# A 96-byte gap that moves the x tiles, chunk 0's weights and the staging tiles of a fused attention and feed-forward kernel

## The chip, the cores and the metric

The kernel runs on one core of one Trainium2 chip. The metric is the device time of one execution in microseconds (us). Three runs of the kernel before took 732.08, 733.01 and 733.45 us; the median is 733.01 us.

## The reference

Attention over 4 batches, 8 heads, 576 positions and a head size of 64, with a bias that a small network computes from the relative position, and behind it a feed-forward layer over the 2304 tokens of 512 values:

```
x_rel = log1p(|i - j|) / log1p(max(i, 1))
bias  = relu(x_rel * w1 + b1) @ w2                 # hidden size 32, one value per head
p     = softmax(q @ k.T / sqrt(64) + bias)
x     = (p @ v), heads side by side                # 2304 x 512, float32
h     = x @ w_in                                   # 512 -> 2048
out   = max(0.01 * h, h) @ w_out                   # 2048 -> 512
```

## The kernel before, in words

The first 318 us compute the bias and the attention; the change doesn't move an operand of TensorE in them. What follows is the feed-forward layer, and that is where the moved tiles are read.

**How it is tiled.** The 2304 tokens are cut into five blocks (`BLOCKS`, L31): blocks 0 to 3 of 512 tokens, block 4 of 256. The 2048 inner values are cut into 16 chunks of 128 (`m`). A pair (n, m) is block n, chunk m. `ffn1(n, m)` (L432 to L442) makes one chunk of h: 12 matmuls, each of which streams a tile of x (512 columns, 256 in block 4) through a stationary 128x128 piece of w_in. `ffn2(n, m)` (L458 to L469) adds the chunk to the output: for each 128 tokens three matmuls (L467, L468, L469), which stream 512 columns of w_out through a stationary piece of the activated chunk, 12 matmuls in a block of 512 tokens and 6 in block 4.

**Why three matmuls for one product.** Every float32 operand is held as two float32r tiles, a high part and the rest: `xh`, `xl` for x, `wih`, `wil` for w_in, `woh`, `wol` for w_out, `gh`, `gl` for the activated chunk. A product is high·high, high·rest and rest·high.

**Order.** The loop at L565 issues for j = 0, 1, ...: `ffn1` of pair j, its activation (`ffn_act`, two ScalarE instructions at L449 and L450, and `ffn_lo`, one VectorE instruction at L456), then `ffn2` of pair j - 2. So TensorE does 12 matmuls of `ffn1`, then 12 of `ffn2` of two pairs earlier, and so on. Ahead of each matmul its weights are loaded (LDWEIGHTS, in the profile the engine PEld); the load for the next matmul starts together with the current one.

**Weights.** All 16 chunks of weights stay in SBUF from block 0 on. While block 0 runs, VectorE and ScalarE still unpack and split the chunks 2 to 15 (`w_abs`, `w_bits`, `w_hi`, `w_lo`, through the staging tiles `raw` and `tmp`): this work stands between the activations of block 0 in the same queues. It is the list `todo` at L542.

**Where the tiles lie.** SBUF has, in each partition, tiles at byte addresses that the pools hand out. The pools on the right side grow downwards from the top. At step n = 8 of the attention (L496 to L503) the pool `gen` is closed, and three pools are opened on the right: `early` (x tiles of even blocks, `x_alloc(early, 0)`, and chunk 0's weights, `w_alloc(early, 0)`), and below it `stage` and `stage_y` (the staging tiles). When the staging is done, the pool `late` takes its place below `early` with the x tiles of odd blocks. The weights of chunks 1 to 14, the `g`, `gh` and `gl` tiles and chunk 15's weights come from pools on the left side, whose first byte is fixed by what lies there. In the kernel before the addresses are, as remainders of the division by 256 and by 512:

| tiles | address of the first | mod 256 | mod 512 |
|---|---|---|---|
| x of even blocks (`xh00`) | 204768 | 224 | 480 |
| x of odd blocks (`xh10`) | 188384 | 224 | 480 |
| weights of chunk 0 (`wih0`) | 221152 | 224 | 480 |
| staging `raw`, `tmp` | 184288, 196576 | 224 | 480 |
| weights of chunks 1 to 15 (`wih1`) | 45184 | 128 | 128 |
| `gh`, `gl` (`gh0`) | 161920 | 128 | 128 |

Every tile of a row is a multiple of 2048 bytes long (staging `raw` 4096), so all of a row have the first one's remainders. A piece of 128 stationary columns begins at a multiple of 512 bytes in its tile, a streamed operand at its tile's first byte. So in `ffn1` of chunk 0 both operands of a matmul have remainder 224, in `ffn1` of the other chunks x has 224 and the weights 128; in `ffn2` of chunk 0 the streamed weights have 224 and the stationary `gh`, `gl` 128, and in `ffn2` of the other chunks both have 128.

The two attention operands of L230 serve as a comparison further on: `qs` (stationary) lies at 66176 and 71296, both 128 mod 512; `ks1` alternates from one unit (a batch and a pair of heads) to the next between 82560 and 87424, which are 128 and 384 mod 512, and `ks2` likewise.

Of the kernel before, what the change touches and what calls it, by code (L numbers as in the profile page):

```python
# [8 lines left out]
F32 = mybir.dt.float32  # L9
# [26 lines left out]
def attention_ffn(ctx: ExitStack, tc: tile.TileContext, qt, kt, vm, vt, wi, wo, cst, out):  # L36
# [37 lines left out]
    def gen_setup():  # L74
        cut = 214 + S - 16 * GEN[0]
        for c in (slice(0, cut), slice(cut, 214 + S)):
            nc.sync.dma_start(out=cs[:, c], in_=cst[:, c])
        nc.vector.memset(warm[:], 0.0)
        nc.scalar.activation(out=warm[:], in_=warm[:], func=AF.Exp)
        nc.vector.tensor_scalar(out=bps[:], in0=psib, scalar1=b1c, scalar2=None, op0=ALU.mult)  # L80
        for c in (slice(0, cut - 214), slice(cut - 214, S)):
            nc.vector.tensor_scalar(out=ltw[:, c], in0=ltw[:, c], scalar1=w1c, scalar2=None, op0=ALU.mult)
        nc.gpsimd.tensor_scalar(out=w2d, in0=w2d, scalar1=8.0, scalar2=None, op0=ALU.mult)
# [60 lines left out]
    def gen_tick(g):  # L144
        if g + 1 < 36:
            gen_r(g + 1)
        if 0 <= g < 36:
            gen_mm(GEN[g])
        if 0 <= g - 1 < 36:
            gen_ev(GEN[g - 1])  # L150
        for c in {16: "0", 24: "1", 27: "M", 34: "2", 37: "3"}.get(g, ()):
            load_bias(0, c)
# [19 lines left out]
    def load_unit(u):  # L172
        hp, b = divmod(u, B)
        q_, k_ = raw_b[u % 2]
        for p in (0, 64):
            nc.sync.dma_start(out=q_[p:p + 64], in_=qt[hp, b])
            nc.sync.dma_start(out=k_[p:p + 64], in_=kt[hp, b])
        raw[u] = (q_, k_)

    def load_v(u):  # L180
        hp, b = divmod(u, B)
        v_ = ap.tile([128, 4, 128], F32, tag="v", name="v", bufs=3)
        nc.sync.dma_start(out=v_[:], in_=vm[hp, b])
        for h in range(2):
            nc.sync.dma_start(out=vt_b[u % 3][64 * h:64 * h + 64, h, :], in_=vt[hp, b, h])
        vv[u] = v_

    def split_hi(u, what):
        q_, k_ = raw[u]
        if what == "q":  # L190
            qs = qs_b[u % 2]
            nc.vector.tensor_copy(qs[:].rearrange("p (a c) -> p a c", a=2)[:, :, 0:S], q_[:].rearrange("p (a c) -> p a c", a=2))
            ks1 = ap.tile([128, KW], F32R, tag="ks1", name="ks1", bufs=2)
            ks2 = ap.tile([128, KW], F32R, tag="ks2", name="ks2", bufs=2)
            qk[u] = (qs, ks1, ks2)
        else:
            nc.vector.tensor_copy(qk[u][1][:], k_[:])
# [175 lines left out]
    def w_alloc(pool, m):  # L373
        wt[m] = [pool.tile([128, DM], F32R, name=f"w{c}{m}") for c in ("ih", "il", "oh", "ol")]

    def x_alloc(pool, i):
        for k in range(KC):
            xs[i, k] = [pool.tile([128, BLK], F32R, name=f"x{c}{i}{k}") for c in "hl"]
# [46 lines left out]
    def w_split(m):  # L425
        for i in range(2):
            w_hi(m, i)
            w_lo(m, i, nc.vector)
# [50 lines left out]
    with tc.manual_schedule():  # L479
        gen_setup()  # L480
        for u in range(2):
            load_unit(u)
            load_v(u)
        sp_ops = [(u, w, a) for u in range(1) for w, a in (("q", None), ("q", 0), ("q", 1), ("k", None), ("k", 0), ("k", 1))]
        done = -1
        early_ops = []
        for n in range(NTILE + LAG + 6):
            u, i = divmod(n, 9)
            if u == 0:
                while done < GEN_AT[i]:  # L490
                    gen_tick(done)
                    done += 1
                    if done >= 6 and done % 2 == 0 and sp_ops:
                        w = sp_ops.pop(0)
                        split_hi(*w[:2]) if w[2] is None else split_lo(*w)
            if n == 8:  # L496
                gen.close()
                early = ctx.enter_context(tc.tile_pool(name="early", bufs=1, side="right"))
                x_alloc(early, 0)
                w_alloc(early, 0)  # L500
                stage, stage_y = ExitStack(), ExitStack()
                pools["s"] = stage.enter_context(tc.tile_pool(name="stage", bufs=1, side="right"))
                pools["y"] = stage_y.enter_context(tc.tile_pool(name="stage_y", bufs=1, side="right"))  # L503
            step(n)
            if n == 13:
                w_fill()
                for m in range(5):
                    early_ops += [(w_abs, m, h) for h in range(2)]
                    early_ops += [(w_bits, m, h, k) for k in range(4) for h in range(2)]
                    if m == 0:  # L510
                        early_ops += [(w_hi, 0, h) for h in range(2)] + [(w_lo, 0, h, nc.vector) for h in range(2)]
            for _ in range({0: 2, 4: 2}.get(i, 0) if n >= 18 else 0):
                if early_ops:
                    f, *args = early_ops.pop(0)
                    f(*args)
            if n == NTILE + 2:
                ffn1(0, 0)
            if u < HP * B:
                if u % B == B - 1 and u // B + 1 < HP:
                    c = {1: "0", 2: "1", 3: "M", 4: "2", 6: "3"}.get(i)  # L520
                    if c:
                        load_bias(u // B + 1, c)
                if u + 1 < HP * B:
                    for f, *args in SPL.get(i, ()):
                        (split_hi, split_lo)[f](u + 1, *args)
                if i == 0 and u + 2 < HP * B:
                    load_unit(u + 2)
                if i == 8 and u + 2 < HP * B:
                    load_v(u + 2)
        att.close()  # L530
        fp = ctx.enter_context(tc.tile_pool(name="ffn", bufs=1, reuse_waits="tile"))
        for m in range(1, MF - 1):
            w_alloc(fp, m)
        for c in ("g", "gh", "gl"):
            gt[c] = [fp.tile([128, BLK], F32 if c == "g" else F32R, name=f"{c}{i}") for i in range(1 if c == "g" else 3)]
        w_split(1)

        def more():
            stage_y.close()
            w_alloc(ctx.enter_context(tc.tile_pool(name="last", bufs=1, reuse_waits="tile")), MF - 1)  # L540

        todo = []  # L542
        for m in range(2, 5):
            todo += [(0, w_hi, m, i) for i in range(2)] + [(0.69, w_lo, m, i, nc.vector) for i in range(2)]
        todo.append((0, more))
        halves_ = [(m, i) for m in range(5, MF) for i in range(2)]
        todo += [(0, w_abs, *t) for t in halves_[:2]]
        for j, t in enumerate(halves_):
            todo += [(0.42, w_bits, *t, 0), (0.43, w_bits, *t, 1)]
            if j:  # L550
                todo.append((0.69, w_lo, *halves_[j - 1], nc.vector))
            todo += [(0.69, w_bits, *t, 2), (0.69, w_bits, *t, 3)]
            todo.append((0, w_hi, *t))
            if j + 2 < len(halves_):
                todo.append((0, w_abs, *halves_[j + 2]))
        todo.append((0.69, w_lo, *halves_[-1], nc.vector))

        def work(budget):
            while todo and budget > 0:
                cost, f, *args = todo.pop(0)  # L560
                f(*args)
                budget -= cost

        seq = [(n, m) for n in range(len(BLOCKS)) for m in range(MF)]
        for j in range(len(seq) + 2):  # L565
            if j < len(seq):
                n, m = seq[j]
                if j:
                    ffn1(n, m)
                work(2.6)  # L570
                ffn_act(n, m)
                work(2.6)
                ffn_lo()
                if (n, m) == (0, MF - 3):
                    assert not todo
                    stage.close()
                    lp = ctx.enter_context(tc.tile_pool(name="late", bufs=1, side="right", reuse_waits="tile"))
                    x_alloc(lp, 1)
                    x_split(1, 0)
                if n + 1 < len(BLOCKS) and m >= MF - (4 if n else 3):  # L580
                    x_split(n + 1, m - MF + 4)
            if j >= 2:
                ffn2(*seq[j - 2])
# [41 lines left out]
```

## Time and profile before

| | |
|---|---|
| median of three runs | 733.01 us |
| profiled execution, from its first to its last instruction | 731.9 us |
| TensorE, matmuls | 710.1 us, 97% of the span |
| VectorE | 394.1 us, 54% |
| ScalarE | 365.6 us, 50% |
| GpSimd | 127.0 us, 17% |
| DMA | 68.26 MB, 93 GB/s over the span |

The page gives for the profiled execution its span, 731.9 us, and no other time of its own; the median of the runs is 1.1 us above it. A matmul's end in the trace is modelled, and matmuls overlap: the duration of one (some 393 ns for 512 columns) is longer than the step from its start to the next one's. How fast TensorE goes is read from the starts.

### The profile page before, as it was taken

To read this page: it belongs to the slowest core of one execution; us is meant where nothing else is said; L and a number is where in the kernel's file an instruction comes from. 1 tells how busy PE (TensorE), PEld (TensorE's weight loads), DVE (VectorE), ACT (ScalarE), POOL (GpSimd) and SP (SyncE) were. 2 spreads that over 40 slices of the span, in tenths; PEclk is the share of its full clock that TensorE was granted. 3 is DMA by queue.
4 is the path that set the end of the run, shared out by engine and by line. 5 is a ranking of instruction groups with operands and counts; after the bars stand their busy time and mean duration, and the time that the engine had idled before them with its cause. 6 is when DMAs were issued, how large, how long until landed. Compare 5 with 4: busy or idle time off the path is not lost.

```text
span 731.9 us, 11398 instructions
## 1 busy us (share of the span) xinstructions
PE 710.1 (97%) x4192; PEld 556.2 (76%) x4192; DVE 394.1 (54%) x1012; ACT 365.6 (50%) x808; POOL 127.0 (17%) x167
## 2 busy tenths in 40 slices
PE   6998999999999999998999999999999999999998
PEld 2347688778878887866877888888888888888896
DVE  7996789789888889759997211122111221112111
ACT  7797777777877777665555221222221231122221
POOL 2104545445544454200000000000000000000000
PEclk9999999999999999999999999999999999999999
DMA  9798848537627950104551010000000010000100
GB/s 211 253 317 229 216 112 243 125 97 218 171 68 183 244 151 18 58 1 144 175 176 52 1 57 1 1 0 28 30 1 1 0 58 1 0 1 0 59 1 30
DMA packets 30263, 68.26 MB, mean 93 GB/s; under 512 B 8192, under 2 KB 8320, under 8 KB 30208
## 3 DMA queue, kind: packets, MB, share of 16 engines
q1 hardware_dynamic: 30208, 67.54, 32.6%
q8 instruction: 33, 0.54, 0.3%
q14 instruction: 22, 0.18, 0.1%
HBM read 51.92 MB, written 15.61 MB: 92 GB/s over the span
## 4 chain that ended last, share of the span: by engine, by line
PE 78%; DVE 15%; DMA 3%; issue 1%; ACT 1%; SPq 0%; POOL 0%; DVEq 0%; POOLq 0%
PE ps_o L441 12%; PE ps_t L441 11%; PE ps_o L335 10%; PE ps_s L230 10%; PE ps_s L468 8%; PE ps_s L467 8%; PE ps_s L469 8%; PE ps_t L295 6%; DVE p L252 2%; DVE tmp L411 2%; DVE tmp L413 2%; DMA raw<-qt 2%; PE ps_o L123 2%; PE ps_t L123 1%; DVE wol L423 1%
## 5 line engine op out<-in xcount | busy, mean ns | idle before, releaser
L456 DVE TENSOR_TENSOR gl<-g,gh 128x512 fp32r<-128x512 f32 (+1 forms) x80 | 51.0, 638 | 270.5 <-ACT g L450 270.5
L230 PE MATMUL ps_s<-ks,qs 128*128 128x288 f32 x640 | 120.3, 314 | 4.5 <-DVE mx L252 4.5
L467 PE MATMUL ps_s<-woh,gh 128*128 128x512 f32 x288 | 113.3, 393 | 1.6 <-ACT g L450 1.6
L469 PE MATMUL ps_s<-woh,gl 128*128 128x512 f32 x288 | 113.1, 393 | 0.9 <-DVE gl L456 0.6
L468 PE MATMUL ps_s<-wol,gh 128*128 128x512 f32 x288 | 113.5, 394 | 0.0
L252 DVE CUSTOM_DVE_ANT_0 p<-ps_s,bias 128x576 f32<-128x576 f32 x128 | 95.0, 751 | 25.9 <-PE ps_s L230 23.1
L260 ACT ACTIVATE p<-p,mx 128x576 f32<-128x576 f32 x128 | 99.9, 780 | 12.9 <-DVE mx L252 11.1
L230 PEld LDWEIGHTS ps_s<-ks,qs 128*128 128x128 f32 x640 | 89.5, 189 | 20.3 <-DVE mx L252 6.4
L311 ACT COPY PT<-ps_t 128x512 f32<-128x512 f32 x128 | 73.7, 577 | 37.5 <-PE ps_t L295 37.5
L449 ACT ACTIVATE gh<-ps_o 128x512 fp32r<-128x512 f32 (+1 forms) x39 | 21.5, 551 | 127.8 <-PE ps_o L441 127.8
L449 ACT ACTIVATE gh<-ps_t 128x512 fp32r<-128x512 f32 (+1 forms) x39 | 21.5, 551 | 114.4 <-PE ps_t L441 114.2
L295 PE MATMUL ps_t<-ident,p 128*128 128x128 f32 x512 | 77.0, 273 | 0.9 <-ACT PT L311 0.8
L335 PE MATMUL ps_o<-PT,v 128*64 128x288 f32 x512 | 69.2, 412 | 0.0
L469 PEld LDWEIGHTS ps_s<-woh,gl 128*128 128x128 f32 x288 | 54.1, 188 | 15.5 <-DVE gl L456 3.5
L467 PEld LDWEIGHTS ps_s<-woh,gh 128*128 128x128 f32 x288 | 54.1, 188 | 14.0 <-ACT g L450 2.0
L295 PEld LDWEIGHTS ps_t<-ident,p 128*128 128x128 f32 x512 | 61.7, 140 | 2.6 <-ACT PT L311 1.8
L468 PEld LDWEIGHTS ps_s<-wol,gh 128*128 128x128 f32 x288 | 54.1, 188 | 11.6
L441 PE MATMUL ps_o<-xh,wil 128*128 128x512 f32 (+1 forms) x156 | 58.4, 375 | 0.0
L441 PE MATMUL ps_t<-xh,wil 128*128 128x512 f32 (+1 forms) x156 | 58.3, 374 | 0.0
L441 PE MATMUL ps_o<-xl,wih 128*128 128x512 f32 (+1 forms) x156 | 58.2, 373 | 0.0
L441 PE MATMUL ps_t<-xl,wih 128*128 128x512 f32 (+1 forms) x156 | 58.2, 373 | 0.0
L441 PE MATMUL ps_o<-xh,wih 128*128 128x512 f32 (+1 forms) x156 | 58.0, 372 | 0.0
(98 smaller groups left out, 1111.8 us busy)
## 6 DMA issues: line engine op xcount, KB each, us to landing
raw<-kt SPq DMA_DIRECT2D x32, 304.0 KB, 5.9
raw<-qt SPq DMA_DIRECT2D x32, 288.0 KB, 5.1
raw<-wi SPq DMA_DIRECT2D x16, 512.0 KB, 3.6
raw<-wo SPq DMA_DIRECT2D x16, 512.0 KB, 3.6
scr<-x SPq DMA_DIRECT2D x21, 295.5 KB, 4.4
bias<-scr SPq DMA_DIRECT2D x16, 288.0 KB, 5.4
out<-x SPq DMA_DIRECT2D x18, 256.0 KB, 2.1
v<-vm SPq DMA_DIRECT2D x16, 256.0 KB, 4.2
```

The costliest lines, as they stand in the source:

```text
L230: nc.tensor.matmul(s_[:, S0 + HS * hh:S0 + HS * hh + HS], qs[:, c0:c0 + 128], ks[:, k0 + HS * hh:k0 + HS * hh + HS], start=(j == 0), stop= ...
L252: nc.vector.tensor_tensor_reduce(out=p, in0=s_[:, S0:S0 + S], in1=bt, scale=-0.125, scalar=3.4e38, op0=ALU.add, op1=ALU.min, accum_out=i)
L260: nc.scalar.activation(out=p, in_=p, func=AF.Exp, bias=i, scale=-1.0, accum_out=sm)
L295: nc.tensor.transpose(t0[:, 128 * jb:128 * jb + 128], p[:, p0 + 128 * jb:p0 + 128 * jb + 128], ident[:])
L311: nc.scalar.copy(out=PT[u, g][:, 0:8, c].rearrange("p (j h) c -> p j h c", h=2)[:, :, h, :], in_=t0[:].rearrange("p (j c) -> p j c", j=4))
L335: nc.tensor.matmul(o[64 * h:64 * h + 64, 0:HS], l, r, start=(jb == 0), stop=(jb == 4))
L441: nc.tensor.matmul(h_[:, :N], w, x[:, :N], start=(j == 0), stop=(j == len(mms) - 1))
L449: nc.scalar.activation(out=gh[:, :N], in_=h_[:, :N], func=AF.Prelu, alpha=0.01)
L456: nc.vector.tensor_sub(gl[:, :N], g[:, :N], gh[:, :N].bitcast(F32))
L467: nc.tensor.matmul(o, gh[:, c], wt[m][2][:], start=(m == 0), stop=False)
L468: nc.tensor.matmul(o, gh[:, c], wt[m][3][:], start=False, stop=False)
L469: nc.tensor.matmul(o, gl[:, c], wt[m][2][:], start=False, stop=(m == MF - 1))
```

## The change

One line is added: a tile of 24 float32 (96 bytes in each partition) in the pool `early`, behind x and chunk 0's weights. No instruction reads or writes it. The pool grows by 96 bytes, so its tiles, and all that lies below it on the right side, begin 96 bytes lower. Nothing else is changed: each engine's instructions stand in the same order as before, with the same waits.

```
                 early = ctx.enter_context(tc.tile_pool(name="early", bufs=1, side="right"))
                 x_alloc(early, 0)
                 w_alloc(early, 0)
+                early.tile([128, 24], F32, name="gap")
                 stage, stage_y = ExitStack(), ExitStack()
```

The addresses after it; rows that aren't here stay as they were:

| tiles | address of the first | mod 256 | mod 512 |
|---|---|---|---|
| x of even blocks (`xh00`) | 204672 | 128 | 384 |
| x of odd blocks (`xh10`) | 188288 | 128 | 384 |
| weights of chunk 0 (`wih0`) | 221056 | 128 | 384 |
| staging `raw`, `tmp` | 184192, 196480 | 128 | 384 |

## Rows read from the trace of the kernel before

**Rows 1.** The page: span, busy time of two engines, granted clock in 40 slices.

```profile
span 731.9 us, 11398 instructions
...
PE 710.1 (97%) x4192; PEld 556.2 (76%) x4192; DVE 394.1 (54%) x1012; ACT 365.6 (50%) x808; POOL 127.0 (17%) x167
...
PEclk9999999999999999999999999999999999999999
```

**Rows 2.** Windows: stretch, its length, busy us of each engine, clock, DMA share.

```profile
410.00:499.10 89.10, 89.10 (x385) 72.15 (x384) 14.78 (x22) 20.58 (x38) 0.00 (x0) 1.00 0.03 12
```

**Rows 3.** Chain of waits, pieces of L441 in blocks 1 to 3: start, us, what.

```profile
493.75 2.81 PE ps_o L441 x12
...
499.33 2.77 PE ps_t L441 x12
...
504.86 2.81 PE ps_o L441 x12
...
510.44 2.82 PE ps_t L441 x12
...
516.05 2.80 PE ps_o L441 x12
...
521.61 2.81 PE ps_t L441 x12
...
588.49 2.77 PE ps_t L441 x12
```

**Rows 4.** Timeline of PE at the very end: start, us, instruction.

```profile
723.98 0.39 PE L467 MATMUL ps_s<-woh,gh 128*128 128x512 f32 x1
...
726.06 0.39 PE L467 MATMUL ps_s<-woh,gh 128*128 128x512 f32 x1
...
726.74 0.39 PE L467 MATMUL ps_s<-woh,gh 128*128 128x512 f32 x1
...
727.42 0.39 PE L467 MATMUL ps_s<-woh,gh 128*128 128x512 f32 x1
```

**Rows 5.** Windows over block 0, columns as in rows 2.

```profile
325.00:394.60 69.60, 67.00 (x280) 52.15 (x281) 67.98 (x128) 39.49 (x70) 0.00 (x0) 1.00 0.47 144
394.60:409.80 15.20, 15.20 (x68) 12.29 (x67) 6.42 (x10) 6.60 (x13) 0.00 (x0) 1.00 0.00 1
```

**Rows 6.** Timeline in block 0, VectorE and the weight load behind it.

```profile
390.13 0.68 DVE L456 TENSOR_TENSOR gl<-g,gh 128x512 fp32r<-128x512 f32 x1
...
390.87 0.19 PEld L469 LDWEIGHTS ps_s<-woh,gl 128*128 128x128 f32 x1 [0.51 <-DVE gl L456]
```

**Rows 7.** Timeline of PE in block 4, first matmuls of chunks.

```profile
677.50 0.28 PE L441 MATMUL ps_t<-xh,wih 128*128 128x256 f32 x1
...
678.93 0.39 PE L467 MATMUL ps_s<-woh,gh 128*128 128x512 f32 x1
...
681.69 0.28 PE L441 MATMUL ps_o<-xh,wih 128*128 128x256 f32 x1
...
683.13 0.39 PE L467 MATMUL ps_s<-woh,gh 128*128 128x512 f32 x1
```

**Rows 8.** Timeline at the start of ffn2 in block 1: eviction and first matmul.

```profile
422.03 0.59 ACT L474 COPY x<-ps_s 128x512 f32<-128x512 f32 x1 [0.45 <-DVE x L476]
423.92 0.39 PE L467 MATMUL ps_s<-woh,gh 128*128 128x512 f32 x1
```

**Rows 9.** VectorE groups between 318 and 420 us: busy us, mean ns.

```profile
L456 DVE TENSOR_TENSOR gl<-g,gh 128x512 fp32r<-128x512 f32 x18 | 12.4, 688 | 17.7 <-ACT g L450 17.7
L423 DVE TENSOR_TENSOR wol<-tmp,woh 128x512 fp32r<-128x512 f32 x15 | 10.3, 686 | 0.7 <-ACT woh L419 0.7
```

**Rows 10.** Waits of engines for the staging DMA: us in total, times, longest.

```profile
ACT tmp L400 <- DMA raw<-wo: 3.5, 10, 0.6
```

**Rows 11.** Windows of L230 alone in two neighbouring units: PE, PEld busy.

```profile
86.30:102.20 15.90, 7.54 (x40) 5.58 (x40) 1.00 0.40 98
102.20:118.10 15.90, 7.52 (x40) 5.60 (x41) 1.00 0.72 192
```

More of the change, by code (lines that the diff above doesn't have):

```diff
@@ L500, in attention_ffn @@
                 w_alloc(early, 0)
+                early.tile([128, 24], F32, name="gap")
                 stage, stage_y = ExitStack(), ExitStack()
```

## The prediction

> **What bounds the kernel now.** I read the page first, to see whether an engine is full: the matmuls are busy for 97% of the 731.9 us, and the granted clock is full (the 2.4 GHz level) in all 40 slices [rows 1]. The windows come next, since a share over the whole span mixes stages. In block 1 TensorE is busy for all of 89.10 us, VectorE for 14.78 and ScalarE for 20.58 [rows 2]; blocks 2 and 3 read alike. So in these blocks nothing but the step from one matmul to the next sets the time. The chain of waits shows these steps by chunk: the reader is to see that one `ffn1` chunk in 16 is shorter. Twelve matmuls take 2.81 us in nearly every chunk, but 2.77 us in (2, 0) and (3, 0), at 499.33 and 588.49 [rows 3]. Chunk 0 is the only one whose w_in has the remainder of x, 224 mod 256 and 480 mod 512. `ffn2` is what lies between two such pieces. Behind 499.33 + 2.77 it takes 2.76 us, and behind 516.05 + 2.80 again 2.76: streamed w_out and stationary `gh`, `gl` agree there. Behind 510.44 + 2.82 it takes 2.79 us: that is `ffn2` of (2, 0), whose w_out has 224 against 128 [rows 3]. Two kinds of matmul, with different tiles and different absolute addresses, tell the same: agreeing operands are faster.
>
> How fast agreeing operands can be is seen where they last longest. The kernel ends with three `ffn2` chunks in a row, 18 matmuls that all agree. The first nine steps, from 723.98 to 726.06, take 2.08 us, 0.231 each; the next six, from 726.06 to 727.42, take 1.36 us, 0.2267 each [rows 4]. So the steps are uneven behind a matmul that disagrees and settle after nine. In block 1 to 3 no run of agreeing matmuls is longer than 12, so they hardly reach the settled state before the next `ffn1` disturbs them. Disagreeing ones cost 2.81/12 = 0.234.
>
> **The change part by part.** The order of the instructions and their waits are the same on every engine; only addresses move.
>
> *Blocks 1 to 3.* Modulo 256, x goes from 224 to 128, where the weights of chunks 1 to 15 are; w_out of chunk 0 goes to 128, where `gh` is. If agreement modulo 256 is what counts, all 384 matmuls of a block agree, with no disturbance from 410.00 to 677.50. A block takes 588.49 - 499.33 = 89.16 us [rows 3]. At the settled step it takes 384 x 0.2267 = 87.05 us. Gain 2.11 us per block, 6.33 us for three. The settled step does hold over a border between chunks: of the 18 matmuls at the end the 13th, at 726.74, is the first of chunk (4, 15), and the steps on both sides of it are 0.227 [rows 4].
>
> *Block 0.* A faster matmul gives nothing while TensorE waits for VectorE. From 325.00 to 394.60 VectorE is busy for 67.98 of 69.60 us, the rest being the short steps between its instructions [rows 5]; it unpacks and splits weights and makes `gl` in the same queue. The last wait for it ends at 390.87: a weight load was idle for 0.51 us until `gl` of (0, 10), begun at 390.13, was there [rows 6]. Whatever TensorE gains before that becomes a longer wait at this place. From 390.87 to 410.00 it runs freely, 19.13 us; at the same rate, 19.13 x 2.11/89.16 = 0.45 us.
>
> *Block 4.* Its `ffn1` streams 256 columns. Chunk 0 (agreeing) takes 678.93 - 677.50 = 1.43 us, chunk 1 (not agreeing) 683.13 - 681.69 = 1.44 us [rows 7]. So matmuls of this width show nothing, and I take 0 for them. The 512-wide matmuls here are 24 of block 3's last two `ffn2` chunks and 96 of block 4, 120 in all. If they settled they would save 120 x (0.231 - 0.2267) = 0.5 us; if the 256-wide ones between them disturb them as now, nothing. I take 0.3, nearer to the upper end as 24 + 18 of them have others of 512 columns ahead.
>
> *What else moves.* The staging tiles go from 224 to 128. The VectorE group with mixed remainders (`wol` from `tmp` at 224 and `woh` at 128) takes 686 ns, the one with all at 128 688 ns [rows 9]: VectorE doesn't respond, cost 0, at most 2 ns x 100 instructions = 0.2 us either way. The staging DMAs write to lower addresses; ScalarE waits 3.5 us in total for them, at most 0.6 at once [rows 10], and this lies beside VectorE's full queue. Bounds for that: 0 to 0.5 us lost. Nothing in the attention reads a moved tile on TensorE: 0.
>
> *What is late next.* At a block's end the accumulators are copied out; the last copy begins at 422.03 and takes 0.59, and the next `ffn2` begins at 423.92 [rows 8]. A faster `ffn1` ahead of it takes 0.1 us of the 1.3 us between. No new wait follows. The copies and the store behind the last matmul stay as they are.
>
> *A rule against it.* The Trainium skill (SBUF — State Buffer, section "Who interferes with whom") gives TensorE two independent read ports, one for the streamed operand and one for weight loads, and says that TensorE waits on nobody. By that, relative addresses are worth nothing, the sum is 0 and the time 733.0 us. The trace doesn't agree: 2.77 against 2.81 us for the same matmuls [rows 3].
>
> **The sum.** 6.33 + 0.45 + 0.3 = 7.1 us. The profiled execution would go from 731.9 to 724.8 us. The median of the runs is 1.1 us above the span, which I keep: 733.0 - 7.1 = 725.9 us.
>
> **The rivals.**
>
> 1. *The period is longer than 256.* All agreeing pairs that this trace holds agree modulo 512 too. After the change x has 384 mod 512 and the weights of chunks 1 to 15 128: half a period apart, should 512 be what counts. `ffn1` would stay at 2.81 us and the time at 733.0 us. Against it stand the attention's matmuls at L230. From one unit to the next `ks` changes from 128 to 384 mod 512 against a fixed `qs`, and 40 matmuls take 7.54 and 7.52 us [rows 11]. That is weak, since these stream 288 columns and the 256-wide ones show no response to a disagreement either [rows 7].
>
> 2. *Addresses aren't the cause.* Something else makes the first chunk of a block quick. Then nothing changes: 733.0 us. Against it: `ffn1` of chunk 0 is quicker than its neighbours and `ffn2` of chunk 0 is slower than its own [rows 3], as agreement has it and as no common cause at a block's start would.
>
> 3. *Each chunk unsettles the next.* The operands agree, but the change between x and w_out starts the uneven steps anew. `ffn1` then takes 2.77 instead of 2.81 us, `ffn2` stays at 2.76. In 89.16 us that is 15 x 0.04 + 0.03 = 0.63 us; from 390.87 to 677.50, 3.2 such blocks, 2.0 us: 731.0 us. For it: every run of 12 starts unevenly now. Against it: the chunk border in rows 4.
>
> 4. *Slower: a remainder of 256 modulo 512 disturbs more than 96 modulo 256 did.* The place is `ffn1` of chunks 1 to 15, 48 of them behind 390.87. No row shows this distance with 512 columns. If the loss against the settled step doubles, from 0.2342 - 0.2267 = 0.0075 to 0.015 us, each chunk takes 0.09 us more: 48 x 0.09 = 4.3 us, 737.3 us. It decides from the point where an `ffn1` step is above 0.2342 on average. For it only speaks that the distance is unseen; against it rows 11.
>
> **How the numbers follow.** The forecast has 0.62: agreement has two independent witnesses, and of the periods that fit them (64, 128, 256, 512; 32 or less doesn't fit, 96 being its multiple) only 512 makes the change miss. Rival 1 has 0.16, rival 2 0.06, rival 3 0.07, rival 4 0.09. A measurement of this kernel tells about 0.2%, 1.5 us, from no change. Forecast and rival 3 are faster: 0.69; rivals 1 and 2 the same: 0.22; rival 4 slower: 0.09. The forecast's own range is 724.6 us (all of block 4 and 1 us of scatter between runs) to 727.2 us (none of block 4, half of block 0, 0.5 lost to staging and the rest scatter). To hold 8 in 10 the range has to take in rival 3 and the greater part of 1 and 2, so its upper end is 733.3 us.
>
> **What would show it.** In the profile after, `ffn1` pieces of the chain in blocks 1 to 3 at 2.72 us, and `ffn2` between them at 2.72 us, a block at 87.05 us instead of 89.16; the waits for `gl` in block 0 somewhat longer and the last of them still at about 391 us; the attention's end at the same time. 2.77 with 2.76 would be rival 3. 2.81 would be rival 1 or 2, more than that rival 4. The forecast is wrong if the 512-wide steps stay above 0.23 us.

## The result and the profile after

The changed kernel took 726.62 us (median of four runs, 725.89 to 727.81), the kernel before 733.23 us beside it. The ratio is 0.9911, with a 95% interval of 0.9897 to 0.9926: 6.6 us less. The prediction was 725.9 us and 7.1 us less. A second set of runs of the same pair, further down, gave 726.15 us and 0.991.

The profile after, in the parts that answer to those of before. First the page (span, busy time, clock), beside [rows 1]:

```profile
span 723.7 us, 11398 instructions
...
PE 703.4 (97%) x4192; PEld 556.7 (77%) x4192; DVE 394.2 (54%) x1012; ACT 365.7 (51%) x808; POOL 127.0 (18%) x167
...
PEclk9999999999999999999999999999999999999999
```

As many instructions, the same clock, the other engines' work unchanged to 0.1 us. The time went out of TensorE's matmuls. Their steps by chunk, from the chain of waits (start, us, what), beside [rows 3]:

```profile
495.44 2.72 PE ps_t L441 x12
500.88 2.72 PE ps_o L441 x12
...
582.48 2.72 PE ps_t L441 x12
...
669.52 1.43 PE ps_t L441 x12
```

The reader is to see three things. Chunk 0 (495.44 and 582.48) is no longer quicker than its neighbours: all have 2.72 us, where chunk 0 had 2.77 and the others 2.81. `ffn2` in between takes 500.88 - 495.44 - 2.72 = 2.72 us too, instead of 2.76. And a block takes 582.48 - 495.44 = 87.04 us instead of 89.16. Block 4's `ffn1`, with 256 columns, stays at 1.43 us (669.52). The single steps, in the timeline of PE across the border from `ffn2` to `ffn1`, beside [rows 4]:

```profile
505.48 0.39 PE L467 MATMUL ps_s<-woh,gh 128*128 128x512 f32 x1
...
506.16 0.39 PE L441 MATMUL ps_t<-xh,wih 128*128 128x512 f32 x1
...
506.84 0.39 PE L441 MATMUL ps_t<-xh,wih 128*128 128x512 f32 x1
```

Six steps in 1.36 us, 0.2267 each, with no disturbance where the chunk changes at 506.16.

In block 0 the quicker step turns into waiting. Waits of the weight loads between 318 and 410 us (us in total, times, longest), first of before, then of after; the list's other rows are equal in both:

```profile
PEld ps_s L469 <- DVE gl L456: 3.5, 6, 0.9
```

```profile
PEld ps_s L469 <- DVE gl L456: 5.0, 8, 1.0
```

The last of these waits, in the timeline of after, beside [rows 6]:

```profile
389.52 0.19 PEld L469 LDWEIGHTS ps_s<-woh,gl 128*128 128x128 f32 x1 [0.62 <-DVE gl L456]
```

From the first `ffn1` matmul (318.34 us before, 317.00 after) to the end of this wait it is 390.87 - 318.34 = 72.53 us before and 389.52 - 317.00 = 72.52 us after: up to here nothing of the quicker step is left.

**The accounts.** From the first `ffn1` matmul to the end the profiled execution took 731.9 - 318.3 = 413.5 us before and 723.7 - 317.0 = 406.7 us after: 6.8 us less. By blocks, from the starts of their first matmuls: block 0 91.66 to 91.24 us (0.42), blocks 1 to 3 89.17 to 87.04 us (2.13 each, 6.38), block 4 and the end 54.37 to 54.33 us (0.04). The spans differ by 1.3 us more, since the profiled execution of before reached the first `ffn1` matmul that much later. This isn't the change's doing, as the experiment `before_again` shows.

### The profile page after: what moved, and what is told of

It reads as the page before. It is cut to its first block, busy times and chain, and to the rows that moved or that the text cites. A ratio compares the mean times of both kernels' runs of the same rounds, so it can differ in the third digit from the quotient of the medians.

```text
span 723.7 us, 11398 instructions
## 1 busy us (share of the span) xinstructions
PE 703.4 (97%) x4192; PEld 556.7 (77%) x4192; DVE 394.2 (54%) x1012; ACT 365.7 (51%) x808; POOL 127.0 (18%) x167
## 4 chain that ended last, share of the span: by engine, by line
PE 80%; DVE 16%; issue 1%; DMA 1%; ACT 1%; SPq 0%; DVEq 0%
PE ps_o L441 11%; PE ps_t L441 11%; PE ps_o L335 10%; PE ps_s L230 10%; PE ps_s L469 8%; PE ps_s L467 8%; PE ps_s L468 8%; PE ps_t L295 7%; DVE p L252 2%; PE ps_o L123 2%; DVE tmp L411 2%; PE ps_t L123 2%; DVE tmp L413 2%; DVE r L112 2%; DVE wol L423 1%
## 5 line engine op out<-in xcount | busy, mean ns | idle before, releaser
L230 PE MATMUL ps_s<-ks,qs 128*128 128x288 f32 x640 | 120.2, 314 | 3.1 <-DVE mx L252 3.1
L230 PEld LDWEIGHTS ps_s<-ks,qs 128*128 128x128 f32 x640 | 89.4, 189 | 18.8 <-DVE mx L252 5.0
L441 PE MATMUL ps_t<-xh,wil 128*128 128x512 f32 (+1 forms) x156 | 57.3, 367 | 0.0
L441 PE MATMUL ps_o<-xh,wil 128*128 128x512 f32 (+1 forms) x156 | 57.3, 367 | 0.0
L441 PE MATMUL ps_t<-xl,wih 128*128 128x512 f32 (+1 forms) x156 | 57.3, 367 | 0.0
L441 PE MATMUL ps_o<-xl,wih 128*128 128x512 f32 (+1 forms) x156 | 57.3, 367 | 0.0
L441 PE MATMUL ps_o<-xh,wih 128*128 128x512 f32 (+1 forms) x156 | 57.3, 367 | 0.0
```

The lines of the kernel that those rows point to most:

```text
L230: nc.tensor.matmul(s_[:, S0 + HS * hh:S0 + HS * hh + HS], qs[:, c0:c0 + 128], ks[:, k0 + HS * hh:k0 + HS * hh + HS], start=(j == 0), stop= ...
L441: nc.tensor.matmul(h_[:, :N], w, x[:, :N], start=(j == 0), stop=(j == len(mms) - 1))
```

## The experiments

The theory: what counts for a matmul of 512 columns is the distance of its streamed operand's address to that of the stationary weights, modulo 256; at distance 0 the steps settle at 0.2267 us. The rivals: another period, absolute addresses, the staging tiles, and in block 0 something other than the supply of weights. Each time stands beside times of the kernel before on the same chip. `map`, `fine`, the three gaps, `before_again` and the two without clamps ran once each; there the argument rests on the steps in their traces and not on the small differences of their times.

### Distances one by one (map, fine)

Two kernels replace everything by chains of 36 matmuls:

```
for i in range(36):
    a, b = s[i % len(s)] // 4, w[i % len(w)] // 4        # byte shifts
    nc.tensor.matmul(p[:, :n], wb[:, b:b + 128], xb[:, a:a + n], start=(i == 0), stop=(i == 35))
```

> This kernel leaves out the whole of attention and feed-forward: it runs 33 chains of 36 back-to-back matmuls (float32r, a weight load each), and its time means nothing. What is read is the length of each chain. Chains 2 to 17 stream 512 columns at 0, 32, 64, ... 480 bytes behind an address with remainder 128 mod 512, with the weights at that remainder; 18 to 20 shift the weights by 96, 128, 256 instead; 21 to 23 alternate the shifts 0 and 96 (both operands together; in opposite phase, so that each streamed operand agrees with the weights being loaded beside it; streamed one alone); 24 to 27 have 288 columns (shift 0, 96, 128, 256), 28 and 29 have 256 columns (0, 96), 30 and 31 repeat 512 columns with 0 and 96. Theory (agreement modulo 256): 36 x 0.2267 = 8.16 us at shifts 0 and 256, 36 x 0.2333 = 8.40 us at 96 and, if only agreement is quick, at all the others; the weights' shift does the same as the streamed one's. Rival with a period of 64 or 128: 8.16 us at 64, 128, 192 ... or at 128, 384 too. Rival with a period of 512: 8.40 us at 256. Rival absolute address (streamed operand on a multiple of 128): shifts of the weights alone change nothing. 256 and 288 columns: no difference between the shifts, 36 x 0.120 = 4.32 us and some 36 x 0.132 = 4.75 us. Of the chains that alternate I expect the one in opposite phase to be quick if the load beside the stream is what matters, the one together if a matmul's own weights are.

The chain of waits of `map`, one piece for each chain of 36 (start, us, what):

```profile
15.84 8.16 PE pb L31 x36
24.00 8.40 PE pa L33 x36
32.41 8.25 PE pb L31 x36
40.66 8.41 PE pa L33 x36
49.07 8.40 PE pb L31 x36
...
82.69 8.19 PE pb L31 x36
...
99.28 8.25 PE pb L31 x36
...
166.37 8.21 PE pb L31 x36
174.58 8.42 PE pa L33 x36
183.00 8.28 PE pb L31 x36
...
199.56 4.74 PE pb L31 x36
...
209.04 4.80 PE pb L31 x36
...
227.21 8.17 PE pb L31 x36
235.38 8.43 PE pa L33 x36
```

Shifts of 0, 32, 64, 96, 128 are the first five rows. 256 (at 82.69) and 320 (at 99.28) repeat 0 and 64: 8.19 and 8.25 us, and the settled steps within the chains are 226.67 ns at 0 and 256 and 228.9 ns at 64 and 320. The other six pairs of shifts that are 256 apart agree to 0.01 us too. So the period is 256, and 512 is out. Weights moved by 256 (166.37) do the same. Weights moved by 96 and by 128 take 8.44 and 8.37 us, where the streamed operand at the same distances (160 and 128 behind the weights) takes 8.43 and 8.40: nearly the same, and the small rest stays unexplained. Repeated at the end, 0 and 96 give 8.17 and 8.43 us. What I hadn't expected is 64, which lies between, at 8.25 us. At 288 columns the shift of 128 costs 0.06 us in 36 (209.04 against 199.56), so those matmuls are nearly deaf to it, and the comparison of units in [rows 11] said little, as the prediction feared.

The chains that alternate don't settle which load counts. Both operands alternating together, so that each matmul agrees with its own weights but not with those being loaded beside it, took 8.42 us (174.58); in opposite phase 8.28 us (183.00); that favours the load beside the stream, but if only that counted, the second should have reached 8.16.

> As with the first map, this leaves out all of attention and feed-forward and runs chains of 36 matmuls of 512 columns; chain 2 on: the streamed operand at 0, 4, 8, ... 252 bytes behind the remainder of the weights, then four that alternate (streamed 0 and 256 with fixed weights; weights 0 and 96 with the streamed operand fixed; 0 and 128 on both together; 0 and 128 in opposite phase). Theory (only full agreement settles at the quickest step): 8.16 us at 0, more at every other shift, 8.40 us at most of them and 8.25 near 64. Rival (there is a still better shift than agreement): a chain below 8.10 us. Alternating 0 and 256: 8.16 us. Weights 0 and 96: 8.28 us, half of the matmuls disturbed. If the load beside the stream is what counts, 0 and 128 together is 8.40 us and in opposite phase about 8.2 us.

Of `fine`, the same view; the shifts of the rows are 0, 20, 28 and 244, and at the end, of the four that alternate, the last two:

```profile
15.96 8.16 PE pb L31 x36
...
57.61 8.64 PE pa L33 x36
...
74.66 8.17 PE pa L33 x36
...
527.33 8.64 PE pa L33 x36
...
568.87 8.23 PE pb L31 x36
577.10 8.29 PE pa L33 x36
```

My expectation was wrong in two points. Agreement is not the only quick distance: seven others of the 64 (28, 60, 156, 236, 240, 252 and, nearly, 76) stay below 8.23 us; the settled step is 226.67 ns at the first six. And 8.40 us (233.33 ns) isn't the length at most of them, but at 22; 16 settle between 228 and 232 ns, 19 above 234. 20, 132, 196 and 244 are slowest, with 240.00 ns. Nothing is below 226.67, so at 512 columns the changed kernel's steps can't be bettered by another distance. The first two chains that alternate came as expected, 8.17 and 8.28 us. The last two, shifts 0 and 128 together and in opposite phase, took 8.23 and 8.29 us: the reverse of what the load beside the stream would give. Which of the two loads counts stays open.

### Other gaps in the kernel (gap32, gap224, gap352)

```diff
-                early.tile([128, 24], F32, name="gap")
+                early.tile([128, 8], F32, name="gap")     # gap32; 56 in gap224, 88 in gap352
```

> A gap of 32 instead of 96 bytes: x and chunk 0's weights at 192 mod 256, the other weights at 128, so the distance is 64. Theory (agreement modulo 256): ffn1 chunks of blocks 1 to 3 as before the change, 2.81 us, a block 89.2 us, the run about 733 us. Rival (the period is 64 or 32): 2.72 us, 87.05 us, about 726 us. Rival (x need only lie on a multiple of 128): as before, 2.81 us.

> A gap of 224 bytes: x and chunk 0's weights at 0 mod 256, the other weights at 128, distance 128. Theory (agreement modulo 256): ffn1 chunks of blocks 1 to 3 at 2.81 us, a block 89.2 us, about 733 us. Rival (period 128): 2.72 us, 87.05 us, about 726 us. Rival (x need only lie on a multiple of 128, whatever the weights do): 2.72 us, about 726 us.

> A gap of 352 bytes: x and chunk 0's weights at 128 mod 512, so all operands agree modulo 512 and not only modulo 256. Theory (agreement modulo 256): every chunk 2.72 us, a block 87.04 us, 726 us, as with the 96 bytes. Rival (256 mod 512 was still a little disturbed): less than 87.04 us per block.

A run of the kernel before took 733.82 us beside them. `gap32` (distance 64) took 730.09, `gap224` (distance 128) 731.36, `gap352` (distance 0 modulo 512 as well) 725.54 us. An `ffn1` piece of block 3's chain for each:

```profile
657.62 2.76 PE ps_o L441 x12
```

```profile
669.36 2.79 PE ps_o L441 x12
```

```profile
663.89 2.72 PE ps_o L441 x12
```

In that order: 2.76, 2.79, 2.72 us. A multiple of 128 (`gap224`) isn't enough, so the rival on x's own alignment falls. Agreement modulo 512 brings nothing over 256: `gap352` has the change's 87.04 us per block (495.09 to 582.13).

The sizes that the theory gave for the other two failed. `gap32` has neither 2.81 nor 2.72 us. For its `ffn1` the map has the reason: distance 64 settles at 0.2289, 12 x 0.2289 = 2.75 us. And a block, from the starts of its first matmuls, is 88.45 us in `gap32` (585.61 to 674.06) and 88.43 us in `gap224` (586.29 to 674.73), not 89.2. Their `ffn1` chunks differ, but so do the `ffn2` chunks between them, the other way: some 2.77 us in `gap32` and 2.74 in `gap224` (2.76 before), though the operands agree in nearly all of these. So what a disagreeing chunk costs the agreeing one behind it depends on the distance as well, in a way that no run explains. In block 4 and the end `gap32` takes 54.00 us, the change 54.33: there, with `ffn1` at 256 columns, another distance is a little better than agreement.

### The other side moved, and the staging alone (left96, stage_all)

```diff
+        fp.tile([128, 24], F32, name="gap")                       # left96, ahead of the weights 1 to 14
         for m in range(1, MF - 1):
             w_alloc(fp, m)
```

> x, chunk 0's weights and the staging stay where the kernel before has them (224 mod 256). Instead the pool of chunks 1 to 14, g, gh, gl and, with it, chunk 15 begins 96 bytes later, so that these go from 128 to 224. Theory (the relative address counts): every 512-wide chunk 2.72 us, a block 87.04 us, the run at 726 to 727 us, as with the change. Rival (the absolute address of x or of the weights counts, 128 being a good one): blocks of 89.2 us or more, 733 us or more. Rival (the staging tiles' move brought the gain): 733 us.

```diff
+                stage.enter_context(tc.tile_pool(name="gapp", bufs=1, side="right")).tile([128, 24], F32, name="gap")
                 pools["s"] = stage.enter_context(tc.tile_pool(name="stage", bufs=1, side="right"))
```

> Only the staging tiles move by 96 bytes (a gap between them and chunk 0's weights); x and all weights stay where the kernel before has them. Theory: no difference, ffn1 chunks 2.81 us, blocks 89.17 us, 733 us (ratio within 0.2% of 1). Rival (staging alignment matters to VectorE or the DMAs): block 0, 91.7 us before, gets shorter, by up to the 1.3 us that the profiled run of the change was ahead at the end of the attention.

`left96`: 726.91 us, ratio 0.992 (0.9903 to 0.9936). `stage_all`: 732.87 us, ratio 0.9998 (0.9989 to 1.0008). The chain in the same stretch, first of `left96`, then of `stage_all`:

```profile
497.63 2.72 PE ps_t L441 x12
503.07 2.72 PE ps_o L441 x12
```

```profile
498.22 2.77 PE ps_t L441 x12
503.76 2.81 PE ps_o L441 x12
```

All operands at 224 are as quick as all at 128: the relative address counts. The staging tiles' move alone brings nothing that shows: block 0 takes 91.58 us, 91.65 before, and the others 89.17.

### Before once more (before_again)

> The kernel before, unchanged, profiled once more: in the profiled run of before the first ffn1 matmul starts at 318.34 us, in those with moved tiles at 316.8 to 317.9 us. Theory (nothing in the attention reads a moved tile; the difference is the scatter of DMA landings at 60 to 75 us): a start anywhere between 316.8 and 318.4 us, blocks of 89.17 us. Rival (the move shortens the attention): 318.3 us again.

The kernel is the one before. The first `ffn1` matmul in the timeline of PE, here and in the profile after:

```profile
317.22 0.48 PE L441 MATMUL ps_s<-xh,wih 128*128 128x512 f32 x1
```

```profile
317.00 0.47 PE L441 MATMUL ps_s<-xh,wih 128*128 128x512 f32 x1
```

Without any move it starts at 317.22 us, not at 318.34. Over the eight profiled executions told of so far (before, after, the gaps, `left96`, `stage_all` and this one) the start lies between 316.81 (`gap352`) and 319.17 us (`left96`), in no order of the addresses. In the slower one of before, the third unit of the attention begins 1.4 us later than in after, behind waits for the landing of `bias` at 66 and 69 us. `left96` moves nothing that the attention reads or writes, and yet it starts 0.8 us later still. So it is scatter, and the span of before is an unlucky one: here it is 730.7 us.

### Where block 0's gain went (pool_lo, after_again, noclamp_before, noclamp_after)

```diff
-                todo.append((0.69, w_lo, *halves_[j - 1], nc.vector))
+                todo.append((0.69, w_lo, *halves_[j - 1], nc.vector if j % 2 == 0 else nc.gpsimd))
```

> The changed kernel, and ten of the 21 subtractions of w_lo that stand between other pieces in todo (0.69 us each on VectorE) go to GpSimd, idle in the feed-forward layer. Theory (in block 0 VectorE's queue, not the matmul step, is what ends last, so that the quicker step could give only 0.4 us there): VectorE gets 6.9 us of free time, the waits for gl (5.0 us, 8 times) all but go, and block 0 shrinks from 91.24 us by some 2 to 4 us towards 87.04 plus the 3 us of its first chunks; 723 to 725 us in all, below the change. Rival (the matmul step or the DMAs bound block 0): 91.2 us still. Rival (GpSimd's subtractions, 1.5 us each in the attention, come late or hold VectorE's reads up): block 0 longer, a new wait of TensorE for wil or wol.

> The changed kernel unchanged, beside the one with GpSimd's part: 726 to 727 us, blocks 1 to 3 of 87.04 us, block 0 of 91.2 us.

`after_again` took 726.15 us, ratio 0.991 (0.9895 to 0.9925). `pool_lo` took 732.32 us, so it lost 6 us, nearly all that the change had brought. (It moved 11 instructions, not ten.) The group of L411 on VectorE between 317 and 420 us (busy us, mean ns), and two of its instructions in the timeline, the second one beside GpSimd's subtraction:

```profile
L411 DVE SCALAR_TENSOR_TENSOR tmp<-raw,tmp 128x512 int32<-128x512 int32 x22 | 26.7, 1214 | 0.4
```

```profile
348.46 0.68 DVE L411 SCALAR_TENSOR_TENSOR tmp<-raw,tmp 128x512 int32<-128x512 int32 x1
...
351.08 1.30 POOL L423 TENSOR_TENSOR wil<-tmp,wih 128x512 fp32r<-128x512 f32 x1 [5.21 <-ACT wih L419]
351.18 1.74 DVE L411 SCALAR_TENSOR_TENSOR tmp<-raw,tmp 128x512 int32<-128x512 int32 x1
```

The mean mixes two kinds: the eleven L411 that run beside a subtraction on GpSimd take some 1.74 us each, the other eleven 0.68 to 0.69, as all 22 do in the changed kernel. That added 26.7 - 15.1 = 11.6 us to VectorE, where 11 x 0.69 = 7.6 us were taken off. The Trainium skill has this (SBUF — State Buffer, section "Who interferes with whom"): a VectorE instruction with two inputs in SBUF contends with a GpSimd instruction that reads SBUF. The trace agrees, with 1.74 against 0.68 us. The last rival came true in its main part, and block 0 took 97.35 instead of 91.24 us; but no new wait for `wil` or `wol` came, it is `gl` that came later. What it does show is that a longer queue on VectorE lengthens block 0: TensorE waited for `gl` 9.8 us instead of 5.0, with the quick step unchanged from 409 us on.

```diff
-            todo += [(0.42, w_bits, *t, 0), (0.43, w_bits, *t, 1)]
+            todo += [(0.42, lambda *a: None), (0.43, w_bits, *t, 1)]     # in the kernel before and in the changed one
```

> The kernel before without the 22 clamps (L407, 0.42 us each on VectorE) that todo has for the weights of chunks 5 to 15: their limiting to a range is left out. Theory (VectorE's queue ends last in block 0): its work per chunk falls from 5.9 us to 5.1 us, under the 5.57 us of TensorE's 24 steps, the waits for gl in chunks 6 to 10 go, block 0 takes 91.66 - 1.8 = 89.9 us, and blocks 1 to 3 stay at 89.17 us.

> The same edit on the changed kernel. Theory (what the quicker step gave in block 0 was hidden behind VectorE): now the quicker step shows there too, block 0 some 1.5 to 2 us shorter than in noclamp_before (it was 0.4 us shorter with the clamps), 88 to 88.4 us, and blocks 1 to 3 at 87.04 us. Rival (the step stays slow in block 0 for another reason, the DMA traffic or the writes of weights): again 0.4 us.

Beside a run of before of 733.34 us they took 732.01 and 725.75 us. The theory's figure for block 0 failed in both. It took 90.82 us in `noclamp_before` (89.9 expected) and 90.40 us in `noclamp_after` (88 to 88.4 expected): 0.42 us apart, as with the clamps. Waits of TensorE's loads for VectorE between 318 and 408.2 us, before and after, and of VectorE for ScalarE between 335 and 394 us in the latter:

```profile
PEld ps_s L469 <- DVE gl L456: 2.7, 6, 0.5
```

```profile
PEld ps_s L469 <- DVE gl L456: 4.0, 7, 0.6
```

```profile
DVE wol L423 <- ACT woh L419: 4.2, 11, 0.7
DVE wil L423 <- ACT wih L419: 3.5, 10, 0.4
```

VectorE did have less to do, but the clamp had stood between a cast on ScalarE and the subtraction that needs its result. Without it VectorE waits there, 7.7 us in all, and from one `gl` to the next it is still 5.89 us, where it was 5.93. The chain of waits of `noclamp_after` goes round accordingly (start, us, what):

```profile
358.58 0.69 DVE tmp L411
359.27 0.60 DVE gl L456
359.87 0.61 DVE tmp L413
...
360.50 0.63 ACT wih L419
...
364.47 0.69 DVE tmp L411
```

So without the clamps it isn't VectorE's busy time but the chain from VectorE over ScalarE's cast and back that paces block 0. The rival's 0.4 us came true, but not for the reason that it gave: the step is quick in block 0 too, while the staging DMAs run. The first matmuls of an `ffn1` chunk there and of the `ffn2` behind it are 2.72 us apart:

```profile
356.52 0.39 PE L441 MATMUL ps_o<-xh,wih 128*128 128x512 f32 x1
...
359.24 0.39 PE L467 MATMUL ps_s<-woh,gh 128*128 128x512 f32 x1
```

The 1.3 us longer wait for `gl` in `noclamp_after` than in `noclamp_before` shows again that the quicker step is spent on waiting. No run here has that chain short enough for the gain to show.

## Why the prediction was right

*Which matmuls disagree, and that agreement counts:* right. The two witnesses in the trace of before (chunk 0's `ffn1` quicker, its `ffn2` slower, [rows 3]) told the cause; `left96`, `stage_all` and the gaps confirm it. The Trainium skill (SBUF — State Buffer, section "Who interferes with whom") calls TensorE's two read ports, for the streamed operand and for weight loads, independent. That addresses are worth nothing, as the prediction drew from it, isn't borne out: `fine` has steps of 226.67 to 240.00 ns for one and the same instruction, by address alone. Where on the chip the two operands get in each other's way no run shows.

*The settled step:* 0.2267 us, read from the last six steps of before [rows 4], became the step of the matmuls in blocks 1 to 3. Predicted 87.05 us per block, measured 87.04; 6.33 us predicted, 6.38 measured. Rival 3 (each chunk unsettles the next) is out: a chunk's border no longer shows.

*Block 0:* 0.45 us predicted, 0.42 measured, the last wait still behind `gl` of (0, 10). VectorE's queue was named rightly as what hides the gain, but that is only a part of it: it was called full because VectorE was busy for 67.98 of 69.60 us [rows 5], and the experiments without the clamps show that the way over ScalarE's cast would hold block 0 at nearly the same pace.

*Block 4:* the one term that was mis-sized. I took 0.3 us; measured 0.04. The timeline of PE in block 4 after the change shows why; the first and last matmul of an `ffn2` chunk, and the first one of the `ffn1` behind it:

```profile
684.79 0.40 PE L467 MATMUL ps_s<-woh,gh 128*128 128x512 f32 x1
...
685.95 0.39 PE L469 MATMUL ps_s<-woh,gl 128*128 128x512 f32 x1
686.18 0.28 PE L441 MATMUL ps_o<-xh,wih 128*128 128x256 f32 x1
```

Six matmuls take 686.18 - 684.79 = 1.39 us, 0.232 each. All operands agree, and yet each chunk begins unevenly behind twelve 256-wide matmuls, as it did before. The nearer end was the lower one. This also corrects the reading of [rows 4], which put the uneven first nine steps down to a matmul that disagrees: 256-wide ones stood ahead of them there too, and at the end of the changed kernel, where all agree, five steps are still uneven (715.81 to 716.97, 1.16 us). In blocks 1 to 3 all matmuls have 512 columns, so the sum for them wasn't touched.

*What else moves:* right. The staging was given 0 to 0.5 us of loss; `stage_all` shows none.

*Rivals 1 and 4:* the map decides. 256 modulo 512 is the same as 0. That matmuls of 288 columns hardly respond made [rows 11] as weak as it was held to be.

*The median:* the sum of 7.1 us less 0.26 for block 4 is 6.8 us, and the two comparisons gave 6.6 and 7.0 us. The 1.1 us that the prediction kept between the span and the median joined two different executions: the profiled execution of after has 725.89 us at a span of 723.7, 2.2 us apart. For the median this cancels. The span was predicted as 724.8 us and came out at 723.7, as that of before was the unlucky one.

## What to carry to other kernels

Where TensorE is back to back, read the step from one start to the next by chunk and look for chunks with the same instructions and another step: the difference may be in the addresses. Between a streamed operand of 512 float32r columns and its weights, equal remainders modulo 256 cost 0.2267 us per matmul, most other distances between 0.2283 and 0.2385 (22 of the 64 measured at 0.2333) and the worst 0.2400; here a gap of 96 bytes in a pool set this without another instruction. Where another engine's chain paces the stage, the same gain only lengthens the wait.

## What the runs showed of the hardware

- The step of a 512-column float32r matmul with its own weight load depends on the distance of the operands' addresses with a period of 256 bytes: 226.67 ns settled at 0, 228.92 at 64, 233.33 at 32, 96 or 128, 240.00 at 20, 132, 196 and 244. 28, 60, 156, 236, 240 and 252 are as quick as 0. What in the chip makes the distance count, and whether a matmul's own weights or those loaded beside it do, isn't shown.
- After a disturbance it took up to nine matmuls until the steps settled, and a run of 256-wide ones is a disturbance even where operands agree (0.232 us in six).
- With 288 columns the settled step is 131.67 ns at 0, 96 and 256 and 133.33 at 128; with 256 columns 120.0 ns at 0 and 96. In `gap32` (distance 64) a chunk of twelve 256-column matmuls takes 1.42 us, in the change 1.43.
- Beside a GpSimd subtraction with two SBUF inputs (1.29 us on average) a VectorE instruction with two SBUF inputs took 1.74 us instead of 0.69.
